# Attention and experts in one kernel: the order of the last tiles, single weight splits, halves at the end, later constants

## The chip, the cores and the metric

One core of one Trainium2 chip runs the kernel. The time is that of one execution in device microseconds. TensorE (PE) multiplies matrices, VectorE (DVE), ScalarE (ACT) and GpSimd (POOL) work on tiles, SyncE (SP) issues loads and stores. Names in brackets are those of the profile.

## The reference

Sliding window attention over 8 batches, 8 heads, 576 positions and head dimension 64, then a mixture of 8 experts over the 4608 tokens, one expert per token, and only for tokens whose skip score is positive:

```
scores = q @ k^T / 8            # where 0 <= i - j < 64, else -1e9
attn   = softmax(scores) @ v    # -> x, 4608 tokens x 512
keep   = x @ w_skip > 0
e      = argmax(x[keep] @ w_gate);  g = softmax(x[keep] @ w_gate)[e]
out    = x;  out[keep] += g * (relu(x[keep] @ w1[e]) @ w2[e])   # 512 -> 1024 -> 512
```

All inputs and outputs are float32.

## The kernel before, in words

The tokens are cut into 36 tiles of 128 (two blocks of 64 positions). A loop over the tiles is a software pipeline. For tile t+1 `score` writes the scores into `ps` (TensorE, line 259; for the first block of a sequence a band of large negative numbers goes ahead of them, line 245). VectorE masks them and takes the maximum (lines 276, 279), and ScalarE makes eight exponentials, one per head (`soften`, line 285); the second four of them are what `softened()` issues. For tile t TensorE transposes the exponentials (296), ScalarE and GpSimd make masked copies `ptm`, and for tile t-1 `tile_out` multiplies with the values (`av`, 444) and VectorE divides (455 to 458). The result x is stored and also transposed (`transpose_x`, 341, tile `px`), copied by ScalarE (346, `xt`) and multiplied with the router's weights (414); for the last tiles ScalarE copies these logits to `lg` (418). `route` then finds expert and gate on VectorE (gmx, gd, gfi, gfm, goh, gohb; 495 to 509), with one exponential on ScalarE (gex, 505), ranks the tokens with the constants `trib`, `cf`, `of` and `base`, and GpSimd scatters token numbers to `lists` in HBM (628).

The tokens of an expert form items, ten in all, of up to three tiles. An item runs in four steps over quarters of the hidden dimension. Per step, `up` makes the product `p` from x and the first weights (three matmuls per slice: high times high 860, low times high 861, high times low 862, here called by line only), ScalarE writes `hh` (917) and VectorE the rest `hl` (920). `down` multiplies with the second weights into `yv`, `yw` or `yu`. Every weight piece (128x1024) is loaded by SP as `raw` (790) and split in two: ScalarE casts the high half `whi` (809), VectorE subtracts to get the low half `wlo` (810). The splits run ahead of their use in a ring of ten; how far ahead, `expert_chunk` decides for each chunk of work with `weights_to(n)`, which issues splits until n pieces are split. At the end of an item `finish` multiplies by the gate and adds x (VectorE, 945), and GpSimd stores the rows indirectly (946). After the last item stands a loop over leftover slots (1395), which is skipped when there are none.

Each engine works through its instructions in the order in which the program wrote them. TensorE's instructions are fetched in blocks of 256, and `tick` counts them. Loads and stores of the attention stage are issued behind fixed instructions of TensorE, just behind the start of a block. The four constants of the router stand in `load_constants` (180 to 187) and are called once, in the loop at t = 1. The first q is loaded by SP behind the first k (1077), the band, the identity `identb` and others by ScalarE's queue (1079 to 1084). The first two items' chunks run in between the last attention tiles; the wait for `transpose_x` there is on the bank of the tile before, since `px` alternates between two banks of tag "t" and the logits of line 414 stand in the same bank as `px`.

Of the kernel before, what the change touches and what calls it, by code (L numbers as in the profile page):

```python
# [10 lines left out]
F32 = mybir.dt.float32  # L11
# [38 lines left out]
AHEAD = 5  # L50
FLYING = 6
# [101 lines left out]
def window_attention_moe(ctx: ExitStack, tc, a, out):  # L153
# [58 lines left out]
    def load_q(n, s=0, e=4):  # L212
# [3 lines left out]
        return nc.sync.dma_start(qs[n][:, s:e], a["qT"][b, :, 4 * g + s : 4 * g + e])  # L216
# [20 lines left out]
    def score(t):  # L237
# [3 lines left out]
        for hf, (_, i) in enumerate(tiles[t]):  # L241
            if i == 0:
                for z in range(2):
                    h = slice(64 * z, 64 * z + 64)
                    tick(2, nc.tensor.matmul(
                        ps[64 * hf : 64 * hf + 64, z, :, 0:64],
                        identb[h, h],
                        band[h].unsqueeze(1).to_broadcast([64, 4, 64]),
                        start=True,
                        stop=True,  # L250
                        skip_group_check=True,
                    ))
        for p in range(4):
            for hf, (_, i) in enumerate(tiles[t]):
                for z in range(2):
# [10 lines left out]
                    ))  # L266
        ss[t] = ps
# [301 lines left out]
    def tick(n, ins):  # L569
        pe[0] += n  # L570
        if pe[0] >= pe[1]:
# [3 lines left out]
            transfers(ins)  # L575
        return ins
# [282 lines left out]
    def mm3(o, lh, ll, rh, rl, first, last):  # L859
        nc.tensor.matmul(o, lh, rh, start=first, stop=False)  # L860
        nc.tensor.matmul(o, lh, rl, start=False, stop=False)  # L861
        nc.tensor.matmul(o, ll, rh, start=False, stop=last)  # L862
# [79 lines left out]
    def finish(y, xg, idx, gate, n=1):  # L942
        m, w = y.shape
        yo = hpool["y"].tile([P, w], F32, name=f"yo{n}", bufs=3 if n == 1 else 1)[:m]
        nc.vector.scalar_tensor_tensor(yo, y, gate, xg[:m], op0=ALU.mult, op1=ALU.add)  # L945
# [12 lines left out]
    def down(it, qi, wh, wl, tags="u", ends=None):  # L958
# [8 lines left out]
        def add(j, f):  # L967
            r = slice(j * P, j * P + it.rows[j])
            w = slice(f * D, (f + 1) * D)
            mm3(it.ys[j], hh[:, f, r], hl[:, f, r], wh[:, w], wl[:, w],  # L970
# [497 lines left out]
```

## Time and profile before

| | us |
|---|---|
| three runs | 416.78, 414.01, 413.55 (median 414.01) |
| profiled execution | 408.61 |
| its span | 407.0 |
| TensorE busy in it | 376.0 |
| VectorE, ScalarE, GpSimd busy | 270.8, 224.4, 178.2 |
| mean granted clock of TensorE | 0.997 |

The profiled execution is one run of its own: 1.61 us lie around its span, and it is 5.4 us shorter than the median of the three runs. TensorE's busy time does not tell how full it is inside a busy stretch, since matmuls overlap; the idle time ahead of an instruction, in brackets behind it, is what can be read. "issue" there means that the profile shows nothing that the engine waited for.

### The profile page before, as it was taken

Reading aid. Unit: us, or ns where it says so; the run is one execution under the profiler, and the core shown is the slowest. Engines: PE = TensorE matmul, PEld = TensorE weight load, DVE = VectorE, ACT = ScalarE, POOL = GpSimd, SP = SyncE. Lnnn points to the kernel's source line nnn. Section 1 sums busy time; section 2 is a strip of 40 time slices with the busy share of each in tenths; the row PEclk is TensorE's granted clock in tenths of the full one; section 3 lists DMA queues with packets and bytes.
Section 4 is the critical chain, followed back from the end, with each engine's and each line's share of the span. In section 5 each row is a group of like instructions: output and inputs, shape, how many; then the busy total and the mean of one; then the engine's idle time right before and its main releaser. Section 6 shows DMA issues by size and latency. Waiting matters only on the chain. (4 is left out here: it accounts for less than half of the span.)

```text
span 407.0 us, 13642 instructions
## 1 busy us (share of the span) xinstructions
PE 376.0 (92%) x5425; PEld 318.1 (78%) x5425; DVE 270.8 (67%) x552; ACT 224.4 (55%) x643; POOL 178.2 (44%) x222
## 2 busy tenths in 40 slices
PE   4879898989889997999999999999999999999993
PEld 3667787767676866898788898888889889888872
DVE  2667778868688856797616789764555566764591
ACT  3767787767667865564315646334425344452670
POOL 5545445467767583475262718116106423010121
PEclk9999999999999999999999999999999999999998
DMA  8988889869877798668738866657657776685460
GB/s 271 321 278 272 284 266 316 299 216 289 279 241 215 220 340 294 200 202 297 275 115 276 263 194 204 209 174 235 217 161 249 262 238 188 207 250 174 156 230 28
DMA packets 40677, 95.68 MB, mean 235 GB/s; under 512 B 7216, under 2 KB 9021, under 8 KB 40604
## 3 DMA queue, kind: packets, MB, share of 16 engines
q1 hardware_dynamic: 33124, 78.21, 59.3%
q0 software_dynamic: 4896, 10.02, 7.5%
q10 hardware_dynamic: 2592, 6.57, 4.8%
q8 instruction: 43, 0.70, 0.7%
q14 instruction: 22, 0.18, 0.1%
HBM read 80.57 MB, written 14.91 MB: 235 GB/s over the span
## 5 line engine op out<-in xcount | busy, mean ns | idle before, releaser
L810 DVE TENSOR_TENSOR wlo<-raw,whi 128x1024 fp32r<-128x1024 f32 x72 | 86.5, 1222 | 24.2 <-ACT whi L809 22.2
L917 ACT ACTIVATE hh<-p 128x256 fp32r<-128x256 f32 (+4 forms) x56 | 22.5, 403 | 94.4 <-PE p L862 91.8
L809 ACT CAST whi<-raw 128x1024 fp32r<-128x1024 f32 x72 | 73.7, 1049 | 0.0
L303 POOL TENSOR_TENSOR ptm<-pm,mask 128x512 f32<-128x512 f32 x36 | 45.9, 1275 | 53.8 <-ACT pm L302 53.6
L860 PE MATMUL p<-x,whi 128*128 128x288 f32 (+5 forms) x224 | 67.4, 301 | 1.8 <-DVE hl L920 1.3
L862 PE MATMUL p<-x,wlo 128*128 128x288 f32 (+5 forms) x224 | 66.0, 295 | 0.6 <-DVE wlo L810 0.6
L861 PE MATMUL p<-x,whi 128*128 128x288 f32 (+5 forms) x224 | 65.8, 294 | 0.0
L285 ACT ACTIVATE s<-ps,nmx 128x64 f32<-128x64 f32 x288 | 62.8, 329 | 1.2
L946 POOL DMA_INDIRECT out<-yo,les x15 | 15.4, 1029 | 95.3 <-DVE yo L945 88.0
L444 PE MATMUL av<-vm,ptm 64*64 64x65 f32 x2048 | 47.4, 223 | 9.2 <-issue 9.1
L920 DVE SCALAR_TENSOR_TENSOR hl<-p,hh 128x256 fp32r<-128x256 f32 (+4 forms) x56 | 24.8, 444 | 46.3 <-ACT hh L917 26.8
L444 PEld LDWEIGHTS av<-vm,ptm 64*64 64x64 f32 x2048 | 39.6, 134 | 16.3 <-issue 14.9
L628 POOL DMA_INDIRECT lists<-ent,gdi x36 | 38.3, 1063 | 19.9 <-issue 12.6
L860 PEld LDWEIGHTS p<-x,whi 128*128 128x128 f32 x224 | 42.2, 188 | 4.7 <-DVE hl L920 1.9
L861 PEld LDWEIGHTS p<-x,whi 128*128 128x128 f32 x224 | 42.2, 188 | 0.9
L862 PEld LDWEIGHTS p<-x,wlo 128*128 128x128 f32 x224 | 42.2, 188 | 0.8 <-DVE wlo L810 0.8
L259 PE MATMUL ps<-k,q 64*64 64x128 f32 (+1 forms) x1024 | 38.5, 274 | 0.9 <-DMA q<-qT 0.4
L276 DVE COPY_PREDICATED ps<-sel,ps 128x512 f32<-128x512 int32 x36 | 24.9, 690 | 18.2 <-PE ps L259 14.0
L346 ACT COPY xt<-px 128x512 f32<-128x512 f32 x36 | 21.2, 589 | 23.8 <-PE px L341 17.6
L259 PEld LDWEIGHTS ps<-k,q 64*64 64x64 f32 x1024 | 31.0, 138 | 4.3 <-issue 2.2
L860 PE MATMUL yv<-whi,hh 128*128 128x512 f32 (+1 forms) x72 | 28.8, 400 | 0.0
L862 PE MATMUL yv<-whi,hl 128*128 128x512 f32 (+1 forms) x72 | 28.2, 392 | 0.0
(188 smaller groups left out, 741.7 us busy)
## 6 DMA issues: line engine op xcount, KB each, us to landing
raw<-wq SPq DMA_DIRECT2D x72, 512.0 KB
vm<-vp SPq DMA_DIRECT2D x32, 260.0 KB
q<-qT SPq DMA_DIRECT2D x32, 256.0 KB
out<-x SPq DMA_DIRECT2D x32, 256.0 KB
k<-kT SPq DMA_DIRECT2D x24, 256.0 KB
w<-wq ACTq DMA_DIRECT2D x12, 512.0 KB
k<-kT SPq DMA_DIRECT2D x8, 384.0 KB
kt<-kT SPq DMA_DIRECT2D x8, 256.0 KB
```

The costliest lines, as they stand in the source:

```text
L259: tick(4, nc.tensor.matmul(ps[64 * hf : 64 * hf + 64, z, p, 64 * w.start :], q[h, p], k[h, w, p], start=True, stop=True, skip_group_check= ...
L276: nc.vector.copy_predicated(cur, sel.unsqueeze(1).unsqueeze(1).to_broadcast([P, 2, 4, 64]), ps[..., :64])
L285: nc.scalar.activation(s[:, q, z], cur[:, z, q], AF.Exp, bias=nmx[:, z, q : q + 1], scale=0.125)
L303: nc.gpsimd.tensor_tensor(part(0, 2), split(pm[:, 0:2], 2), kept(2), op=ALU.mult)
L444: ins = tick(4, nc.tensor.matmul(av[64 * hf : 64 * hf + 64, z, q * VW : (q + 1) * VW], ptm[h, q, 2 * hf + 1 - w], win[hf][w][h, q], start= ...
L628: ins = nc.gpsimd.indirect_dma_start(out=lists, out_offset=bass.IndirectOffsetOnAxis(ap=di, axis=0), in_=ent.bitcast(I32), in_offset=None, ...
L809: nc.scalar.copy(hi, raw)
L810: nc.vector.tensor_tensor(lo, raw, hi.bitcast(F32), op=ALU.subtract)
L860: nc.tensor.matmul(o, lh, rh, start=first, stop=False)
L861: nc.tensor.matmul(o, lh, rl, start=False, stop=False)
L862: nc.tensor.matmul(o, ll, rh, start=False, stop=last)
L920: beat(nc.vector.scalar_tensor_tensor(hl[:, f, :m], p1[:, :m], 0.0, hh[:, f, :m].bitcast(F32), op0=ALU.max, op1=ALU.subtract))
```

## The change

Five things are altered.

1. The first q goes out on ScalarE's queue, first there, and the band on SP's; for tile 0 the band's matmuls stand behind the scores.
2. `load_constants` is a generator. From the fourth block on, `tick` takes one load of it at each block boundary: cf, the lists' zeros, of, trib. GpSimd's copy of `base` moves from t = 5 to t = 10.
3. At t = 34 the second four exponentials stand behind the cast of the first item's x and the copy of the logits. The first weight split of the stage stands ahead of the transpose of tile 33, and the last two transposes write to a bank of their own ("late", tag "u").
4. In `expert_chunk` the lead of the splits is bounded: a chunk splits what it needs now and otherwise one piece at most, and where the ring is short nothing but what it needs now.
5. The last step of the last item makes its output in two halves of 256 columns. Each half is multiplied by the gate as soon as it is there, and one store follows both.

```diff
     def load_constants():
-        nc.sync.dma_start(cf, a["c_f"])
-        nc.sync.dma_start(of, a["c_first"])
-        nc.sync.dma_start(trib, a["c_tri"])
-        nc.sync.dma_start(
+        yield nc.sync.dma_start(cf, a["c_f"])
+        yield nc.sync.dma_start(
             lists[:LPAD].rearrange(...), a["c_list"].rearrange(...),
         )
+        yield nc.sync.dma_start(of, a["c_first"])
+        yield nc.sync.dma_start(trib, a["c_tri"])
+
+    constant = load_constants()
...
+        if t:
+            banded()
         for p in range(4):
...
+        if not t:
+            banded()
...
-        px = psum.tile([P, NDC, P], F32, name="px", tag="t", bufs=2)
+        if t < NT - 2:
+            px = psum.tile([P, NDC, P], F32, name="px", tag="t", bufs=2)
+        else:
+            px = banks["late"].tile([P, NDC, P], F32, name="px", tag="u", bufs=1)
...
             transfers(ins)
+            if pe[1] > FETCH + QUIET * BLOCK:
+                load = next(constant, None)
+                if load is not None:
+                    behind(load, ins)
...
-        nc.vector.scalar_tensor_tensor(yo, y, gate, xg[:m], op0=ALU.mult, op1=ALU.add)
+        c = slice(0, w) if half is None else slice(half * w // 2, (half + 1) * w // 2)
+        nc.vector.scalar_tensor_tensor(yo[:, c], y[:, c], gate, xg[:m, c], op0=ALU.mult, op1=ALU.add)
+        if half == 0:
+            halved.append(yo)
+            return
...
-            for j in range(it.nt):
+            for half in range(2):
                 for f in range(2):
-                    add(j, f)
-                finish(it.ys[j], it.xg[j], it.idx[j], it.gate[j])
+                    add(0, f, half)
+                finish(it.ys[0], it.xg[0], it.idx[0], it.gate[0], half=half)
...
-        for f in (load_k, load_q):
-            after_load(f(0, 0, 2), 1)
-        nc.scalar.dma_start(band, a["c_band"])
+        after_load(load_k(0, 0, 2), 1)
+        after_load(load_q(0, 0, 2, nc.scalar), 1)
+        nc.sync.dma_start(band, a["c_band"])
...
-            if t == 1:
-                load_constants()
-            if t == 5:
+            if t == 10:
                 nc.gpsimd.tensor_copy(base, cf[:, off["base"]])
...
-                softened()
+                if t < NT - 2:
+                    softened()
                 if t >= FIRSTX:
                     its[0].split(xhl[0], t - FIRSTX, "t")()
                 if t - LAG[t] >= SINGLY:
                     logits(t - LAG[t])
+                if t == NT - 2:
+                    softened()
...
-                eager = 0 if short[0] or gathered[0] < 3 else min(ptr["split"] + RATE, ptr["free"] + min(RING, len(ring)) - 1)
-                weights_to(max(need, eager))
+                lead = ptr["free"] + min(RING, len(ring)) - 1 if gathered[0] >= 3 else need + 2
+                weights_to(now if short[0] else max(now, min(lead, ptr["split"] + RATE)))
...
-        transpose_x(NT - 3)
         weight_split(ptr["split"])
         ptr["split"] += 1
+        transpose_x(NT - 3)
```

On ScalarE, at t = 34, the eight exponentials `s` of the last tile stood ahead of the cast of x and the logits' copy `lg`; then came the copy `xt` of tile 33 and the first split of the stage. Before:

```order
L285 ACTIVATE s<-ps,nmx 128x64 x8
L850 CAST x_150<-px_3691 128x4x128
L418 COPY lg<-px 128x9
L346 COPY xt_3618<-px 128x4x128
L809 CAST whi_146<-raw_140 128x1024
L418 COPY lg<-px 128x9
```

Now:

```order
L294 ACTIVATE s<-ps,nmx 128x64 x4
L866 CAST x_150<-px_3687 128x4x128
L430 COPY lg<-px 128x9
L294 ACTIVATE s<-ps,nmx 128x64 x4
L825 CAST whi_146<-raw_140 128x1024
L358 COPY xt_3618<-px 128x4x128
L430 COPY lg<-px 128x9
```

Four exponentials, and the copy `xt`, have moved behind.

On VectorE, between the products' rests `hl` of the first item and its next x, the low halves of the third and fourth piece stood ahead of the router's work on the last group of tiles (`gmx` to `gohb`). Before:

```order
L920 SCALAR_TENSOR_TENSOR hl<-p_3921,hh 128x256
L810 TENSOR_TENSOR wlo_3719<-raw_142,whi_3718 128x1024
L810 TENSOR_TENSOR wlo_3721<-raw_143,whi_3720 128x1024
L920 SCALAR_TENSOR_TENSOR hl<-p_3948,hh 128x256
L495 TENSOR_REDUCE gmx<-lg 128x6
L497 TENSOR_TENSOR gd<-lg,gmx 128x48
L500 SCALAR_TENSOR_TENSOR gfi<-gd,cf 128x48
L502 TENSOR_REDUCE gfm<-gfi 128x6
L507 TENSOR_TENSOR goh<-gfi,gfm 128x48
L509 SCALAR_TENSOR_TENSOR gohb<-lg,goh 128x48
```

Now:

```order
L936 SCALAR_TENSOR_TENSOR hl<-p_3921,hh 128x256
L936 SCALAR_TENSOR_TENSOR hl<-p_3942,hh 128x256
L507 TENSOR_REDUCE gmx<-lg 128x6
L509 TENSOR_TENSOR gd<-lg,gmx 128x48
L512 SCALAR_TENSOR_TENSOR gfi<-gd,cf 128x48
L514 TENSOR_REDUCE gfm<-gfi 128x6
L519 TENSOR_TENSOR goh<-gfi,gfm 128x48
L521 SCALAR_TENSOR_TENSOR gohb<-lg,goh 128x48
L826 TENSOR_TENSOR wlo_3719<-raw_142,whi_3718 128x1024
L869 TENSOR_TENSOR x_3992<-px_4025,x_3992 128x4x128
L826 TENSOR_TENSOR wlo_3721<-raw_143,whi_3720 128x1024
```

The low half of the third piece has moved behind six of the router's operations, that of the fourth behind the rest of x. On ScalarE the two casts moved in the same way: behind `hh`, `lg` and `gex`. Further on, where four casts in a row stood between two pairs of `hh`, there are three, since three earlier ones have closed up.

At the very end, the loop over leftover slots (the rows with a jump, and the body ahead of them) stands between the last item's work and the program's end. GpSimd has the last item's store, from `yo_6648`, behind the loop both before and now:

```order
L1395 REGISTER_ALU
L1395 COMPARE_AND_BRANCH
L1395 UNCONDITIONAL_BRANCH
L946 DMA out<-yo_6648,les 4608x512
L1465 UNCONDITIONAL_BRANCH
```

VectorE, which before had the whole product ahead of the loop and nothing behind it, now has the second half's product there:

```order
L967 SCALAR_TENSOR_TENSOR yo_6850<-yu,lel,xg_115 128x512
L1422 REGISTER_ALU
L1422 COMPARE_AND_BRANCH
L1422 UNCONDITIONAL_BRANCH
L967 SCALAR_TENSOR_TENSOR yo_6648<-yv,les,xg_118 104x256
L1492 UNCONDITIONAL_BRANCH
```

The first half's product stays ahead of the loop. The four loads of constants stood in a row on SP's queue between loads of q and of vm; each now stands alone, the first of them thirteen rows of that queue further on, with four or five rows between two of them. TensorE's order is otherwise as it was, but for tile 0 and the twelve matmuls of half width.

## Rows read from the trace of the kernel before

**Rows 1.** The page's busy time: engine, us, share of the span, instructions.

```profile
PE 376.0 (92%) x5425; PEld 318.1 (78%) x5425; DVE 270.8 (67%) x552; ACT 224.4 (55%) x643; POOL 178.2 (44%) x222
```

**Rows 2.** Busy time by stage: window, busy us (instructions) by engine, clock, DMA share, GB/s.

```profile
20.00:30.00 10.00, 7.55 (x251) 6.36 (x251) 6.49 (x14) 6.90 (x28) 4.02 (x5) 1.00 0.80 266
...
150.00:160.00 10.00, 7.78 (x221) 6.53 (x213) 6.51 (x17) 6.15 (x20) 5.21 (x7) 1.00 0.95 348
...
160.00:170.00 10.00, 8.84 (x133) 7.90 (x134) 6.39 (x19) 4.71 (x10) 3.09 (x3) 1.00 0.77 249
...
200.00:300.00 100.00, 99.60 (x627) 87.22 (x627) 59.91 (x106) 41.95 (x74) 39.33 (x56) 1.00 0.65 210
```

**Rows 3.** TensorE's waits: what waited, for what; us in total, times, longest.

```profile
PE av L444 <- issue: 10.0, 19, 2.1
...
PE px L341 <- DVE hl L920: 0.5, 1, 0.5
...
PE p L860 <- issue: 0.5, 1, 0.5
```

**Rows 4.** The start, in order of time: start us, us, engine, line, operation, tiles, count [idle].

```profile
4.57 0.42 PE L245 MATMUL ps<-band,identb 64*64 64x256 bf16 x2 [4.57 <-DMA identb<-c_identb]
...
7.08 1.88 PE L259 MATMUL ps<-k,q 64*64 64x128 f32 x32 [0.43 <-DMA q<-qT]
```

**Rows 5.** In order of time, SP's queue and TensorE, 17 to 24 us.

```profile
17.14 0.83 SPq L184 DMA_DIRECT2D lists<-c_list  x1
...
23.24 0.40 PE L444 MATMUL av<-vm,ptm 64*64 64x65 f32 x13 [2.12 <-issue]
```

**Rows 6.** In order of time, ScalarE and TensorE at the transition, 154 to 161 us.

```profile
154.20 1.75 ACT L285 ACTIVATE s<-ps,nmx 128x64 f32<-128x64 f32 x8
...
154.90 0.64 PE L414 MATMUL px<-wg,xt 128*64 128x9 f32 x16
...
156.37 0.17 ACT L418 COPY lg<-px 128x9 f32<-128x9 f32 x1
...
156.59 0.66 PE L341 MATMUL px<-ident,x 128*128 128x128 f32 x4 [1.05 <-ACT lg L418]
...
160.12 0.39 PE L862 MATMUL p<-x,wlo 128*128 128x256 f32 x1 [0.57 <-DVE wlo L810]
```

**Rows 7.** In order of time, the third split and what reads it, 169 to 174 us.

```profile
169.16 2.00 ACT L809 CAST whi<-raw 128x1024 fp32r<-128x1024 f32 x2
...
171.57 0.17 ACT L418 COPY lg<-px 128x9 f32<-128x9 f32 x1
...
172.13 0.28 PE L862 MATMUL p<-x,wlo 128*128 128x256 f32 x1
...
172.86 0.19 DVE L495 TENSOR_REDUCE gmx<-lg 128x6 f32<-128x48 f32 x1
...
173.33 0.25 ACT L505 ACTIVATE gex<-gd 128x48 f32<-128x48 f32 x1 [1.59 <-DVE gd L497]
```

**Rows 8.** In order of time, four low halves in a row, 192 to 198 us.

```profile
192.86 4.63 DVE L810 TENSOR_TENSOR wlo<-raw,whi 128x1024 fp32r<-128x1024 f32 x4 [0.51 <-ACT whi L809]
...
197.88 0.40 PE L860 MATMUL p<-x,whi 128*128 128x288 f32 x1 [0.88 <-DVE hl L920]
```

**Rows 9.** The end; VectorE's drain behind the loop; an earlier product and its store.

```profile
399.13 0.39 PE L860 MATMUL yv<-whi,hh 128*104 128x512 f32 x1
...
400.71 0.75 DVE L945 SCALAR_TENSOR_TENSOR yo<-yv,les,xg 104x512 f32<-104x512 f32 x1 [2.02 <-PE yv L862]
...
402.73 1.02 POOL L946 DMA_INDIRECT out<-yo,les  x1 [5.82 <-issue]
...
L1465 DVEq DRAIN  x2: 10/14/17, 403.2 to 406.4; - x2
...
243.89 0.75 DVE L945 SCALAR_TENSOR_TENSOR yo<-yw,les,xg 128x512 f32<-128x512 f32 x1
...
244.94 1.15 POOL L946 DMA_INDIRECT out<-yo,les  x1 [4.68 <-DVE yo L945]
```

More of the change, by code (lines that the diff above doesn't have):

```diff
@@ L50 @@
 AHEAD = 5
+QUIET = 3
 FLYING = 6
@@ L210, in load_k, with load_q @@
         return nc.sync.dma_start(ks[n % NKB][:, s0 : e + 1], a["kT"][b, :, 4 * g + s0 - 1 : 4 * g + e])
-    def load_q(n, s=0, e=4):
+    def load_q(n, s=0, e=4, queue=nc.sync):
         b, g = divmod(n, 2)
@@ L240, in score, with banded @@
         win = windows(t)
[L241 to L252, printed above, removed]
+        def banded():
+            for hf, (_, i) in enumerate(tiles[t]):
+                if i == 0:
+                    for z in range(2):
+                        h = slice(64 * z, 64 * z + 64)
+                        tick(2, nc.tensor.matmul(
+                            ps[64 * hf : 64 * hf + 64, z, :, 0:64],
+                            identb[h, h],
+                            band[h].unsqueeze(1).to_broadcast([64, 4, 64]),
+                            start=True,
+                            stop=True,
+                            skip_group_check=True,
+                        ))
+        if t:
+            banded()
         for p in range(4):
@@ L857, in split_x, with mm3 @@
         return rest
[L859 to L862, printed above, removed]
+    def mm3(o, lh, ll, rh, rl, first, last, **kw):
+        nc.tensor.matmul(o, lh, rh, start=first, stop=False, **kw)
+        nc.tensor.matmul(o, lh, rl, start=False, stop=False, **kw)
+        nc.tensor.matmul(o, ll, rh, start=False, stop=last, **kw)
     class Item:
@@ L940, in up, with finish @@
             yield 1.3
-    def finish(y, xg, idx, gate, n=1):
+    halved = []
+    def finish(y, xg, idx, gate, n=1, half=None):
         m, w = y.shape
-        yo = hpool["y"].tile([P, w], F32, name=f"yo{n}", bufs=3 if n == 1 else 1)[:m]
-        nc.vector.scalar_tensor_tensor(yo, y, gate, xg[:m], op0=ALU.mult, op1=ALU.add)
+        if half:
+            yo = halved.pop()
+        else:
+            yo = hpool["y"].tile([P, w], F32, name=f"yo{n}", bufs=3 if n == 1 else 1)[:m]
+        c = slice(0, w) if half is None else slice(half * w // 2, (half + 1) * w // 2)
[3 more added lines that the diff above has]
+            return
         ins = nc.gpsimd.indirect_dma_start(
@@ L965, in down, with add @@
                 it.ys.append(y[: it.rows[j]] if j < it.full else y[:, 0:P])
-        def add(j, f):
+        def add(j, f, half=None):
             r = slice(j * P, j * P + it.rows[j])
-            w = slice(f * D, (f + 1) * D)
-            mm3(it.ys[j], hh[:, f, r], hl[:, f, r], wh[:, w], wl[:, w],
-                qi == 0 and f == 0, qi == NQ - 1 and f == 1)
+            c = slice(0, D) if half is None else slice(half * D // 2, (half + 1) * D // 2)
+            w = slice(f * D + c.start, f * D + c.stop)
+            mm3(it.ys[j][:, c], hh[:, f, r], hl[:, f, r], wh[:, w], wl[:, w],
+                qi == 0 and f == 0, f == 1 and qi == NQ - (2 if it is its[-1] and half is None else 1), **({} if half is None else {"skip_group_check": True}))
         if qi == NQ - 1 and it is its[-1]:
             tables["more"] = nc.values_load(tables["left"][0:1, 0:1], min_val=0, max_val=NSLOT)
-            for j in range(it.nt):
+            for half in range(2):
                 for f in range(2):
-                    add(j, f)
-                finish(it.ys[j], it.xg[j], it.idx[j], it.gate[j])
+                    add(0, f, half)
+                finish(it.ys[0], it.xg[0], it.idx[0], it.gate[0], half=half)
             return
```

2 lines of the change are left out of this document (1 added, 1 removed).

## The prediction

> **What bounds the kernel now.** The page's busy line comes first: TensorE works 376.0 us of the 407.0 us span [rows 1], so 31 us of idle TensorE are all that a reordering can win, and no instruction of weight is taken away here. The table by stage says where those 31 us lie [rows 2]. From 200 to 300 us TensorE is busy for 99.60 of 100 us, and the 100 us after it read the same, so the long expert stage has nothing to give. Idle time sits at the start, in the attention stage (7.55 of 10 us busy at 20 to 30), at the transition from attention to experts (7.78 and 8.84 of 10 us between 150 and 170), and behind the last matmul. The granted clock is 1.00 in every one of these windows, so no term below is a matter of the clock. The list of TensorE's waits [rows 3] then names the largest: "issue" ahead of the attention-times-values matmuls, 10.0 us in 19 pieces, the longest 2.1 us, which leaves a mean of (10.0 - 2.1) / 18 = 0.44 us for the others. These pieces come once per block of 256 of TensorE's instructions. Two waits of 0.5 us, for hl and before a product of the first expert item, lie in the transition.
>
> **The start.** TensorE first moves at 4.57 us, when the identity for the band arrives, and the scores follow [rows 4]. Now the scores stand first and q goes out on ScalarE's queue as its first load, instead of second on SP's. What the scores need, k and q, is 512 KB with the same bytes in flight, so they can begin about 0.2 us earlier at best. But the second tile's scores wait for their own q until 7.08 us [rows 4], and nothing puts that load ahead of where it was. I take -0.1 us, bounds -0.3 (band and identity wholly off the path) and +0.2 (q second to land because two queues share the engines).
>
> **The constants.** Four loads stand on SP's queue one behind the other, the last, the lists, issued at 17.14 for 0.83 us [rows 5]. From their shapes they are 256, 83, 32 and 32 KB. At the 266 GB/s of the window at 20 to 30 us [rows 2], 403 KB are 1.5 us of transfers. TensorE's longest pause, 2.12 us, ends at 23.24 [rows 5], and I read it as the fetch of instructions that stood behind them. If it falls to about 1.0, because q, k and v loads still queue there, 1.1 us go. Given back: the four loads now stand behind one fetch boundary each, cf, then the lists, the other two. The lists alone are 256 KB / 266 GB/s = 1.0 us of the queue, just before a later fetch; the small ones cost 0.1 to 0.3 us each. I take 0.6 us of new pauses, less than the 1.5 us of bytes because each comes alone: -1.1 + 0.6 = -0.5 us. Bounds: -1.7 (the pause falls to the mean 0.44 and nothing comes back) and +0.8 (nothing goes, the lists and the small ones lengthen later pauses by 0.8). GpSimd's copy of the base moves five tiles later with cf and still stands well ahead of the router that reads it: nothing.
>
> The row shows the longest pause right behind the loads, and shows no more than that. The Trainium skill, "DMA: Bandwidth & Descriptors", section "Queues, rings and completion order", says that each DMA engine takes turns between the queue rows it has work for, a packet from each; "Runtime: NRT & Kernel Launch", section "Instruction fetch mechanics", calls the crossing of a block "mostly hidden". By these an instruction fetch on its own queue would not stand behind SP's loads, this term would be 0 and the sum -0.5.
>
> **The transition, tile 34.** Before, all eight exponentials run on ScalarE from 154.20 for 1.75 us; then the cast of x and the copy of the logits (156.37), and only behind that copy could TensorE transpose the next x, at 156.59 after 1.05 us idle [rows 6]. Now the second four exponentials (0.87 us) stand behind cast and copy, and the transpose has a bank of its own. Cast and copy move up by 0.87 us, but the logits' matmuls end at 154.90 + 0.64 = 155.54 [rows 6], so I move the transpose to 155.83: -0.76. The weight split now stands ahead of the transpose's copy, so the wait for the low half at 160.12 (0.57) falls to about 0.3: TensorE is 1.02 ahead. The two waits of 0.5 us [rows 3] stood for hl, made late by the same work, and go too: 2.0 us ahead. Followed through by hand in the new order, with the transposes out of the way of the tile before, it is 2.36 us just before 169.1.
>
> **One split per chunk.** The four splits that stood in pairs come one at a time. The third split's cast ran at 169.16 as one of two (2.00 us for both, so 1.00 each), and TensorE read its low half at 172.13 [rows 7]. Now it stands on ScalarE behind hh, the logits' copy and the router's exponential, and on VectorE behind six router operations. The logits' copy of the last tile, at 171.57 [rows 7] before, comes at 169.2 by the gain above. From there 0.17 for the copy, then two small VectorE operations and ScalarE's exponential, 0.72 us from 172.86 to 173.58 as they followed each other before [rows 7], then 1.00 for the cast and 1.16 for the low half (4.63 / 4 [rows 8]), with a tenth between them: 172.35. TensorE, 2.36 us ahead, is stopped, and goes on 0.2 us later than before. So the whole gain of the paragraph above is lost again here: +0.2 net. VectorE's next work, hl of that step, is not late by it, since it stands ahead of the split.
>
> Further on the four casts in one block, with the low halves from 192.86 to 197.49 [rows 8], become three. hl waits behind them, and TensorE 0.88 us for hl at 197.88 [rows 8]. One low half less is 1.16 us, more than the wait: -0.88. The transition gives +0.2 - 0.9 = -0.7. Bounds: -3.3, if the split is not late, and +0.6, if the transpose did not hang on the copy and only a third of the 0.88 goes. From 200 us on each step has work for a split in its shadow, and the order there is unchanged: 0.
>
> **The end.** The last six matmuls start at 399.13 and VectorE's product waits for them until 400.71, 1.58 us; it takes 0.75 [rows 9]. In halves the first six take half the columns: 0.85, so the first product starts at 399.98 and takes 0.45 (between 0.38, half of 0.75, and 0.75). But the second half shares the bank and waits for it, and VectorE's second product stands behind the branch that skips the loop. Before, VectorE's product ended at 401.46 and its next instruction behind the loop came at 403.2 [rows 9]: 1.74 us. So the second product starts at 400.43 + 1.74 = 402.17 and ends 402.6. GpSimd's store follows its product by 0.30 us where it waits for one (243.89 + 0.75 to 244.94) [rows 9]: 402.9, against 402.73. +0.2 us; bounds 0 and +0.6 (first product 0.75).
>
> **Sum.** -0.1 - 0.5 - 0.7 + 0.2 = -1.1 us against the profiled execution's own 408.61 us (its span 407.0), so 407.5. The median of the three runs, 414.01, stands 1.3% above that execution; I carry the same amount over: 413.0 (rounded up from 412.9).
>
> **Rivals.**
> *Late split with no lead.* If the transpose waited at 156.59 for the logits' matmuls and not for ScalarE, TensorE has no 2.36 us to lose. The chain from the copy at 171.57 then lands at 171.57 + 0.17 + 0.72 + 2.16 + 0.1 = 174.72 instead of 172.13: +2.6; with the burst's -0.9 and the end's +0.2 that is +1.9, or 415.9, and 416.7 if the constants cost their worst. For it speaks that the copy at 156.37 stood behind two things, matmuls and cast; against it, that those matmuls had ended 0.8 us before [rows 6]. It decides if TensorE's transpose of tile 33 stays within 0.2 us of its old distance to the exponentials. Chance 0.2, and 0.05 of it beyond +1%, by pauses that pile up.
> *Waits gone for good.* The split finds room and the 2.36 us stay: -3.3, with constants -1.7, start -0.3 and end +0.2: -5.1, or 408.9. The windows at 150 to 170 us hold 3.4 us of idle time in all [rows 2], so nothing larger is to be had. Against it: the order of both engines puts the split last. Chance 0.15.
> *Fetches do not hang on the loads.* A pause ends with the arrival of instructions, and the loads beside it are coincidence: constants 0, the rest as summed, -0.6, or 413.4. Chance 0.2: the long pause stands once, just there, which speaks against it; the two sections above speak for it.
> The forecast has 0.45.
>
> **Range and chances.** One per cent is 4.1 us, about what a measurement of this kernel can tell from no change. The forecast's own bounds with the spread of the three runs (413.55 to 416.78) give 411 to 415; to the rivals on both sides it reaches 409.5 to 416.3. Only the second rival, with its terms near their ends, lies below 409.9: faster 0.15. Beyond 418.1 lies the late split with everything else at its worst: slower 0.05. The rest, 0.80, is within one per cent.
>
> **What would show it.** Right: the pause near 23 us falls to about 1 us while one near 43 grows; the transpose follows the logits' matmuls at once; TensorE stands idle some 2.5 us before the first product with the third split's low half; the wait at 197.88 is gone; VectorE's second product starts about 1.74 us behind the end of its first. Wrong: TensorE between 160 and 180 us as full as at 200, a longest pause that stays at 2 us, or a second product within 0.5 us of the last matmul's data.

## The result, and the profile after

The change is slower. In the runs taken against the kernel before its ratio is 1.0137, 95% interval 1.0099 to 1.0176; the median of its six runs is 416.88 us (416.27 to 419.65), against 413.73 us (411.46 to 416.78) for six of the kernel before. A ratio leaves out the runs that lie more than 1.5% above the fastest of their kernel, a median counts them all. The plain ratio of these medians is 1.0076 and that of the means 1.0092, so the 1.0137 is rather high. Taken again in two later studies, it gave 1.0074 (1.0042 to 1.0105) and 1.0097 (1.0062 to 1.0131). The forecast was 413.0 us with a range to 416.3; the time lies just above that range.

The profiled execution took 416.83 us, its span 415.2. That is 8.2 us over the 407.0 of the kernel before, more than the runs' ratio gives: that kernel alone has medians of 407.2 us in some studies below and 413.3 in others, so only distances inside one trace are compared. The page's busy line hardly moves, 379.6 us for TensorE instead of 376.0:

```profile
PE 379.6 (91%) x5431; PEld 325.1 (78%) x5431; DVE 271.5 (65%) x553; ACT 225.1 (54%) x643; POOL 181.9 (44%) x222
```

The table by stage, with the columns of [rows 2] (the clock stands third from the end):

```profile
20.00:30.00 10.00, 9.25 (x295) 8.11 (x292) 8.17 (x19) 7.70 (x31) 4.73 (x5) 1.00 0.87 282
150.00:160.00 10.00, 7.77 (x209) 6.63 (x203) 6.69 (x18) 6.34 (x21) 5.42 (x7) 0.90 0.91 313
160.00:170.00 10.00, 10.00 (x139) 9.75 (x137) 5.89 (x16) 3.30 (x9) 2.04 (x2) 0.76 0.61 206
170.00:180.00 10.00, 7.04 (x52) 6.36 (x51) 5.48 (x12) 4.84 (x10) 7.53 (x8) 0.75 0.37 108
180.00:190.00 10.00, 10.00 (x66) 9.10 (x66) 8.06 (x25) 5.04 (x10) 5.73 (x6) 0.91 0.62 200
190.00:200.00 10.00, 10.00 (x64) 9.25 (x64) 9.51 (x18) 7.45 (x11) 5.62 (x4) 1.00 0.90 305
200.00:300.00 100.00, 98.61 (x621) 86.70 (x620) 60.59 (x109) 41.16 (x73) 40.30 (x57) 1.00 0.65 214
```

Two things are new. The clock, 1.00 in every window of [rows 2], is 0.75 to 0.91 in four windows between 150 and 190 us: a window that reads "10.00 busy" at 0.76 is not a full window. And 170 to 180 us holds 3 us of idle time. TensorE's list of waits names it:

```profile
PE av L456 <- issue: 10.8, 17, 1.7
...
PE p L876 <- ACT whi L825: 2.5, 1, 2.5
...
PE px L865 <- DMA xg<-out,les: 1.1, 1, 1.1
...
PE px L353 <- ACT lg L430: 0.9, 1, 0.9
...
PE p L878 <- DVE wlo L826: 0.5, 1, 0.5
```

The wait for whi, the cast of a split, is in no list of TensorE's waits of the kernel before. In order of time, ScalarE, VectorE and TensorE around it (compare [rows 7]):

```profile
171.54 0.64 PE L426 MATMUL px<-wg,xt 128*64 128x9 f32 x16
172.11 0.66 PE L865 MATMUL px<-ident,xg 128*128 128x128 f32 x4
173.35 0.17 ACT L430 COPY lg<-px 128x9 f32<-128x9 f32 x1 [1.32 <-PE px L865]
174.03 0.24 ACT L517 ACTIVATE gex<-gd 128x48 f32<-128x48 f32 x1 [0.51 <-DVE gd L509]
174.18 1.03 ACT L825 CAST whi<-raw 128x1024 fp32r<-128x1024 f32 x1
175.24 1.23 DVE L826 TENSOR_TENSOR wlo<-raw,whi 128x1024 fp32r<-128x1024 f32 x1 [0.27 <-ACT whi L825]
175.26 0.58 PE L876 MATMUL p<-x,whi 128*128 128x256 f32 x1 [2.49 <-ACT whi L825]
176.52 0.58 PE L878 MATMUL p<-x,wlo 128*128 128x256 f32 x1 [0.46 <-DVE wlo L826]
```

The split's cast starts at 174.18, behind the logits' copy and the router's exponential, and TensorE stands still for 2.49 us, makes two products with the high half, and stands still for 0.46 more, for the low half. Single microseconds tell what comes behind that stop:

```profile
174.00:175.00 1.00, 0.00 (x0) 0.00 (x0) 0.84 (x4) 0.97 (x2) 0.99 (x1) 0.99 0.00 0
175.00:176.00 1.00, 0.74 (x2) 0.50 (x2) 0.76 (x1) 1.00 (x3) 0.69 (x2) 0.50 0.03 1
...
180.00:181.00 1.00, 1.00 (x7) 1.00 (x7) 0.59 (x1) 0.86 (x2) 0.70 (x2) 0.50 0.77 226
181.00:182.00 1.00, 1.00 (x7) 1.00 (x6) 1.00 (x2) 0.00 (x0) 1.00 (x1) 0.59 0.60 231
```

For the 6 us behind the stop TensorE runs at the lower level, 1.2 GHz (0.50), with seven matmuls in a full microsecond. The same fall stands from 158 to 164 us, behind the wait at tile 33. There, in order of time (compare [rows 6]):

```profile
154.60 0.93 ACT L294 ACTIVATE s<-ps,nmx 128x64 f32<-128x64 f32 x4
155.30 0.64 PE L426 MATMUL px<-wg,xt 128*64 128x9 f32 x16
156.66 0.17 ACT L430 COPY lg<-px 128x9 f32<-128x9 f32 x1 [0.65 <-PE px L426]
156.72 0.94 ACT L294 ACTIVATE s<-ps,nmx 128x64 f32<-128x64 f32 x4
156.88 0.66 PE L353 MATMUL px<-ident,x 128*128 128x128 f32 x4 [0.94 <-ACT lg L430]
```

Four exponentials are indeed gone from in front of the copy, yet ScalarE now stands 0.65 us idle for the matmuls, and the transpose comes 1.58 us behind the logits' start instead of 1.69 [rows 6].

The start (compare [rows 4, 5]) and the end (compare [rows 9]), in order of time:

```profile
4.72 1.34 PE L266 MATMUL ps<-k,q 64*64 64x64 f32 x26 [4.72 <-DMA q<-qT]
...
9.13 1.47 PE L305 MATMUL pt<-ident,s 128*128 128x128 f32 x4 [0.96 <-DMA ident<-c_ident]
...
18.79 0.74 PE L456 MATMUL av<-vm,ptm 64*64 64x65 f32 x35 [1.52 <-issue]
...
23.09 0.40 PE L456 MATMUL av<-vm,ptm 64*64 64x65 f32 x13 [0.75 <-issue]
...
406.11 0.28 PE L876 MATMUL yv<-whi,hh 128*104 128x256 f32 x1
...
407.01 0.48 DVE L967 SCALAR_TENSOR_TENSOR yo<-yv,les,xg 104x256 f32<-104x256 f32 x1 [1.34 <-PE yv L878]
...
409.20 0.48 DVE L967 SCALAR_TENSOR_TENSOR yo<-yv,les,xg 104x256 f32<-104x256 f32 x1 [1.71 <-PEq L1422]
409.99 1.03 POOL L971 DMA_INDIRECT out<-yo,les  x1 [6.11 <-DVE yo L967]
```

### The profile page after: what moved, and what is told of

Its sections match the earlier page's. It is cut to its first block, busy times and chain, and to the rows that moved or that the text cites. A ratio compares the mean times of both kernels' runs of the same rounds, so it can differ in the third digit from the quotient of the medians.

```text
span 415.2 us, 13659 instructions
## 1 busy us (share of the span) xinstructions
PE 379.6 (91%) x5431; PEld 325.1 (78%) x5431; DVE 271.5 (65%) x553; ACT 225.1 (54%) x643; POOL 181.9 (44%) x222
## 5 line engine op out<-in xcount | busy, mean ns | idle before, releaser
L876 PE MATMUL p<-x,whi 128*128 128x288 f32 (+5 forms) x224 | 69.0, 308 | 2.5 <-ACT whi L825 2.5
L878 PE MATMUL p<-x,wlo 128*128 128x288 f32 (+5 forms) x224 | 67.6, 302 | 0.5 <-DVE wlo L826 0.5
L877 PE MATMUL p<-x,whi 128*128 128x288 f32 (+5 forms) x224 | 67.4, 301 | 0.0
L644 POOL DMA_INDIRECT lists<-ent,gdi x36 | 40.5, 1125 | 21.2 <-issue 14.4
L876 PEld LDWEIGHTS p<-x,whi 128*128 128x128 f32 x224 | 43.9, 196 | 4.5 <-ACT whi L825 2.7
L877 PEld LDWEIGHTS p<-x,whi 128*128 128x128 f32 x224 | 43.9, 196 | 0.9
L878 PEld LDWEIGHTS p<-x,wlo 128*128 128x128 f32 x224 | 43.7, 195 | 0.8 <-DVE wlo L826 0.8
L876 PE MATMUL yv<-whi,hh 128*128 128x512 f32 (+2 forms) x74 | 29.3, 395 | 0.6 <-DVEq L1422 0.6
L878 PE MATMUL yv<-whi,hl 128*128 128x512 f32 (+2 forms) x74 | 28.6, 386 | 0.0
```

What stands on the lines that cost most here:

```text
L644: ins = nc.gpsimd.indirect_dma_start(out=lists, out_offset=bass.IndirectOffsetOnAxis(ap=di, axis=0), in_=ent.bitcast(I32), in_offset=None, ...
L876: nc.tensor.matmul(o, lh, rh, start=first, stop=False, **kw)
L877: nc.tensor.matmul(o, lh, rl, start=False, stop=False, **kw)
L878: nc.tensor.matmul(o, ll, rh, start=False, stop=last, **kw)
```

## The experiments

**Theory.** The third split, placed behind the router (the "late split"; "early" is its old place), stops TensorE, and the lower clock behind the stop makes it dearer. **Rivals:** the constants' loads or the start; the end in halves ("whole" is the old form); the tile-34 order itself.

The runs form five studies; each ratio is to the kernel before in the same study. That kernel took 407.2 us in the first two studies and 413.3, 413.2 and 412.3 in the others (medians).

**First study: one part undone or alone.** `e1` is the change with the split back ahead of the router:

```diff
-                weights_to(now if short[0] else max(now, min(lead, ptr["split"] + RATE)))
+                weights_to(need if short[0] else max(now, min(lead, ptr["split"] + RATE)))
```

> The changed kernel, with the third and fourth split back ahead of the router's work on the last tiles (where the ring is short a chunk splits what the next one needs, as before the change); all else as changed. Late-split theory: the 2.49 us wait for the third split's high half and the 0.46 us for its low half go, TensorE has no pause long enough for the clock to fall at 175 us, and the kernel is 4 to 6 us faster than the change, 411 to 413 us beside a before of 413.7. Rival, the clock falls at the transition whatever the split does (it also fell at 158 us, ahead of the split): the wait goes, the time falls by 1 to 2 us only, 415 to 416. Rival, the loss comes from start, constants or end: no more than 1 us.

`e2` is the kernel before with the late split alone:

```diff
-                weights_to(max(need, eager))
+                weights_to(now if short[0] else max(need, eager))
```

> The kernel before with the late split alone: where the ring is short a chunk splits only what it needs now. Late-split theory: slower than before by 2.5 us of waiting and up to 3.5 us for the clock behind it, 416 to 420 us, with a pause of 2 to 5 us ahead of the third split's first product. Rivals (clock falls anyway, or other parts): within 1.5 us of before.

`e3` is the kernel before with the constants taken one per block, `e4` the change with its last output in one piece:

```diff
-            if t == 1:
-                load_constants()
-            if t == 5:
+            if t == 10:
...
+            if pe[1] > FETCH + QUIET * BLOCK:
+                load = next(constant, None)
```

> The kernel before with the four constants' loads alone moved, one per block, and the base's copy at tile 10. The forecast's term: 0.5 us faster, the pause near 23 us at about 1 us. If fetches do not hang on loads: within 0.2 us of before, the long pause still there or elsewhere. If it is a part of the loss: 1 us or more slower. From the delays read in the two traces (the attention stage 0.7 to 1.4 us ahead from tile 7 to tile 32): 0.7 to 1.4 us faster.

```diff
-            for half in range(2):
-                for f in range(2):
-                    add(0, f, half)
-                finish(it.ys[0], it.xg[0], it.idx[0], it.gate[0], half=half)
+            for f in range(2):
+                add(0, f)
+            finish(it.ys[0], it.xg[0], it.idx[0], it.gate[0])
```

> The changed kernel with the last output in one piece as before. From the trace of the change, whose second product started at 409.20, 1.71 us behind the end of the first: 0.5 to 1.5 us faster than the change, 415.5 to 416.5 us. If the halves gained: slower than the change.

Measured: `e1` 1.0032 (0.9982 to 1.0082), `e2` 1.0050 (1.0007 to 1.0094), `e3` 0.9957 (0.9894 to 1.0020), `e4` 1.0023 (0.9977 to 1.0069). The late split alone makes the kernel before slower; the constants don't. Undoing the split took the wait for whi away, but `e1` did not become faster than before. Its list of TensorE's waits shows another one further on:

```profile
PE px L865 <- DMA xg<-out,les: 2.3, 1, 2.3
```

By single microseconds, with the clock third from the end:

```profile
205.00:206.00 1.00, 0.21 (x1) 0.22 (x2) 0.00 (x0) 0.00 (x0) 0.00 (x0) 0.93 0.25 81
206.00:207.00 1.00, 1.00 (x6) 1.00 (x6) 0.00 (x0) 0.09 (x1) 0.42 (x3) 0.50 0.00 0
207.00:208.00 1.00, 1.00 (x6) 1.00 (x6) 0.47 (x1) 0.50 (x1) 0.36 (x3) 0.50 0.05 16
```

There too the clock falls behind the stop. TensorE waits for the gather of the third item's rows, which GpSimd issues behind the load of its list; that list comes from the scatters behind the router.

**Second study.** `e5` is the change once more, without an edit. `e6` has the edits of `e1` and `e4` together. `e7` fills the stop: the transposes ahead of it are made six times over, with the same output. The condition also held at two later items, where they are plain extra work. `e8` is the kernel before with the halves alone.

> The change itself, unaltered, beside the others of this call on one chip. If the loss on the first chip (ratio 1.0137) is the kernel's: 1.008 to 1.018. From the two single parts measured so far (late split alone 1.005, the change with a whole end 1.0023): 1.005 to 1.008.

> The change with both undone: third and fourth split early again and the last output in one piece; what stays is the first q, the constants, tile 34 and one split per chunk. If late split and halves are the loss: no slower than before, ratio 0.994 to 1.001, about 4 us faster than the change. If start or tile 34 lose as well: over 1.002.

```diff
-        for c in range(NDC):
+        for c in (i % NDC for i in range(NDC * (6 if xg is its[1].xg[0] else 1))):
```

> The change with the wait for the third split filled: the four transposes of the second item's first tile are made six times over into the same place, 20 matmuls of some 0.12 us in the 2.5 us in which TensorE had nothing. If the half clock behind the wait costs time: TensorE stays at 1.00 between 174 and 182 us, what was 6.4 us at half clock runs in 3.2, and the kernel is 2 to 3 us faster than the change although it does more. If only the wait costs: the same as the change within 0.5 us.

```diff
...
-            for j in range(it.nt):
+            for half in range(2):
                 for f in range(2):
-                    add(j, f)
-                finish(it.ys[j], it.xg[j], it.idx[j], it.gate[j])
+                    add(0, f, half)
+                finish(it.ys[0], it.xg[0], it.idx[0], it.gate[0], half=half)
```

> The kernel before with the last output in halves alone. From the two traces: from VectorE's last hl to the end of the span the change took 1.2 us more, so 1.0 to 1.3 us slower than before, 1.0025 to 1.003. The forecast's term: 0.2 us slower, 1.0005. If overlapping the halves gains: faster.

Measured: `e5` 1.0074 (1.0042 to 1.0105), `e6` 1.0035 (0.9999 to 1.0071), `e7` 1.0080 (1.0042 to 1.0118), `e8` 1.0041 (1.0008 to 1.0075). The halves alone cost time, though the interval comes close to 1. `e7` decides nothing, since it carries the later extra work. `e6` waits 2.5 us for the same gather.

**Third study.** `e9` fills the stop once only. `e10` is the kernel before with the new start, `e11` with the tile-34 order, `e12` with one split per chunk but the third one early.

```diff
+    filled = []
...
-        for c in range(NDC):
+        more = 1 if xg is not its[1].xg[0] or filled else 6
+        filled.extend([0] * (more - 1))
+        for c in (i % NDC for i in range(NDC * more)):
```

> The change with the filling of the wait for the third split at that one place only (the kernel before this repeated it at two later items, where 40 matmuls cost 2 to 5 us of a full TensorE). If the half clock behind the wait costs time: 1.5 to 3 us faster than the change, ratio to before 1.000 to 1.004, unless TensorE then waits longer for the third item's gather near 205 us, which would leave 1.003 to 1.006. If the half clock costs nothing: 1.0074 as the change.

```diff
-        for f in (load_k, load_q):
-            after_load(f(0, 0, 2), 1)
-        nc.scalar.dma_start(band, a["c_band"])
+        after_load(load_k(0, 0, 2), 1)
+        after_load(load_q(0, 0, 2, nc.scalar), 1)
+        nc.sync.dma_start(band, a["c_band"])
```

> The kernel before with the start alone: first q by ScalarE's queue, band by SP's, tile 0's band behind its scores. The forecast's term: 0.1 us faster, lost in the noise (0.998 to 1.002). From the traces of the change, where the first transposes waited 0.96 us for the identity and the clock fell right behind: 0.5 to 1.5 us late at tile 3, made up by tile 10 since loads set the pace there, so also 0.998 to 1.002. If it persists: 1.003.

```diff
+            px = banks["late"].tile([P, NDC, P], F32, name="px", tag="u", bufs=1)
...
-                softened()
+                if t < NT - 2:
+                    softened()
...
+                if t == NT - 2:
+                    softened()
...
-        transpose_x(NT - 3)
         weight_split(ptr["split"])
         ptr["split"] += 1
+        transpose_x(NT - 3)
```

> The kernel before with the last tiles' order alone: second four exponentials of the last tile behind cast and logits' copy, split ahead of the transpose, own bank for the last two transposes. The forecast's terms: up to 2.4 us ahead when the third split is read, and that stands early here, so 1.5 to 2.4 us faster, 0.994 to 0.997. If TensorE then waits for the third item's gather, which GpSimd's scatters set: 0.998 to 1.002, with a wait of 2 us or more ahead of that item's transposes.

```diff
-                weights_to(max(need, eager))
+                weights_to(need if short[0] else max(now, min(lead, ptr["split"] + RATE)))
```

> The kernel before with one split per chunk alone, but with what the next chunk needs where the ring is short, so that the third split stays early. The forecast's term: the wait of 0.88 us for hl near 198 us goes, 0.9 us faster, 0.998. If the gather near 205 us sets the pace: the same as before, 0.998 to 1.002, the wait moved there.

Measured: `e9` 1.0090 (1.0045 to 1.0135), `e10` 0.9989 (0.9949 to 1.0028), `e11` 0.9939 (0.9895 to 0.9982), `e12` 1.0009 (0.9965 to 1.0054). In this study the tile-34 order is the one part with a gain that can be told from nothing. In `e9` the clock holds through the place where it fell. In order of time, TensorE there:

```profile
175.83 2.84 PE L869 MATMUL px<-ident,xg 128*128 128x128 f32 x24
179.00 0.39 PE L880 MATMUL p<-x,whi 128*128 128x256 f32 x1 [0.33 <-issue]
180.26 0.39 PE L882 MATMUL p<-x,wlo 128*128 128x256 f32 x1 [0.76 <-DVE wlo L826]
```

And by single microseconds:

```profile
175.00:176.00 1.00, 1.00 (x21) 0.84 (x20) 0.21 (x1) 0.38 (x1) 0.69 (x2) 1.00 0.46 146
...
181.00:182.00 1.00, 1.00 (x11) 1.00 (x11) 0.94 (x1) 0.25 (x1) 0.69 (x2) 1.00 0.78 131
```

The fall follows this stop: behind it the clock is at 0.50 in the traces of all seven kernels with the late split and no filling, and at 1.00 at that place in `e7`, `e9` and all eleven with the split early. The runs of `e9` do not show the gain, however. Its ratio, 1.0090, is not below the 1.0074 that its expectation gave for a clock that costs nothing; but the interval, 0.45% to either side or 1.9 us, is too wide to tell that from the 1.5 us which the traces give. What the clock alone costs rests on traces and stays open in the runs.

**Fourth study.** `e13` is the kernel before with constants and tile-34 order (the edits of `e3` and `e11`), `e14` is `e6` again, `e15` the kernel before with tile-34 order and late split (`e11` and `e2`), `e16` the change a third time.

> The kernel before with the two parts that gained alone, the constants one per block (0.9957) and the last tiles' order (0.9939); splits, start and end as before. If the gains add: 0.988 to 0.993. If both only bring TensorE earlier to the third item's gather: 0.994 to 0.997, as the better one. If they were chance: 0.998 to 1.002.

> The change with the third and fourth split early and the last output in one piece, a second time, on the chip of the others of this call. If 1.0035 was right: 1.001 to 1.006, and one split per chunk takes back what the last tiles' order gives. If the parts add (start 0.9989, constants 0.9957, tile 34 0.9939, one split 1.0009): 0.988 to 0.994.

> The kernel before with the last tiles' order and the late split, nothing else. If the late split, bound to the router's chain, takes whatever lead TensorE has and adds its wait: 1.003 to 1.008, 0.9 to 1.4 per cent above the last tiles' order alone. If the two are independent: 0.9939 x 1.005 = 0.999.

> The change itself once more, beside these: 1.007 to 1.014, as on the first two chips. If late split and halves are its loss, it stands 0.6 to 1.2 per cent above the kernel with both undone.

Measured: `e13` 0.9976 (0.9942 to 1.0010), `e14` 1.0003 (0.9974 to 1.0033), `e15` 1.0063 (1.0024 to 1.0102), `e16` 1.0097 (1.0062 to 1.0131). The tile-34 order with the late split is slower than the kernel before, where two independent parts would have given 0.999; in the same study `e13`, with the split early, is not. By their single ratios the start, the constants, the tile-34 order and single splits (third one early) would give 0.989 together. `e6` and `e14`, which have these four, are at 1.0035 and 1.0003: most of what the parts seem to gain is not there in their sum, and no run shows why. The change loses 0.94% against `e14`, which differs from it by the split and the halves alone. In `e15`, where the clock was whole until the stop, the list of TensorE's instructions has the pattern of the change:

```profile
170.07 0.64 PE L417 MATMUL px<-wg,xt 128*64 128x9 f32 x16
...
173.82 0.58 PE L863 MATMUL p<-x,whi 128*128 128x256 f32 x1 [2.52 <-ACT whi L812]
...
175.08 0.58 PE L865 MATMUL p<-x,wlo 128*128 128x256 f32 x1 [0.46 <-DVE wlo L813]
```

**Fifth study.** `e17` is `e11` again, `e18` is `e4` again.

> The last tiles' order alone on the kernel before, a second time, as the version that would beat both kernels. If 0.9939 was right: 0.990 to 0.997. If it was chance, as the 0.9976 with the constants suggests: 0.997 to 1.001.

> The change with the last output in one piece but the third split late, a second time. If the late split on top of the last tiles' order costs 0.6 to 1.2 per cent and the halves the rest of the change's loss: 1.004 to 1.007, between the change (1.0097) and the change with both undone (1.0003). If the halves are all of it: 0.999 to 1.002.

Measured: `e17` 0.9953 (0.9909 to 0.9996), `e18` 1.0076 (1.0034 to 1.0118). The gain of the tile-34 order is not safe. `e11` has it in ratio and medians (411.27 against 413.25), but the medians of `e17` and of the kernel before beside it, 412.29 and 412.28, are the same, and the interval of `e13` reaches 1.0010. With the whole output and the late split the kernel is slower here; as `e4` the same program had 1.0023 (0.9977 to 1.0069), which left that open.

**The transition in distances.** Each is the difference of two start times in one trace, in us: from the logits' matmuls of tile 33 to those of the last tile (A), from these to the logits' copy (B), from that copy to the first product with a low half behind the stop (C), from there to the sixth hl of the expert stage (D), from the third hl to the sixth (E), from the sixth to the twentieth (F).

| | A | B | C | D | E | F |
|---|---|---|---|---|---|---|
| before | 15.87 | 0.80 | 0.56 | 4.92 | 8.39 | 54.33 |
| the change | 16.24 | 1.81 | 3.17 | 6.14 | 12.46 | 54.81 |
| `e16`, the change | 14.02 | 1.81 | 3.17 | 6.09 | 12.42 | 54.92 |
| `e5`, the change | 16.67 | 0.69 | 3.16 | 6.37 | 11.57 | 54.84 |
| `e15`, tile 34 and late | 13.34 | 1.84 | 3.17 | 5.88 | 12.23 | 54.71 |
| `e9`, stop filled | 13.90 | 1.83 | 3.17 | 4.60 | 10.94 | 54.33 |
| `e11`, tile 34 | 13.90 | 1.33 | | | 8.39 | 55.69 |
| `e6`, early, whole | 13.21 | 1.32 | | | 8.38 | 56.88 |
| `e12`, one split, early | 15.84 | 0.80 | | | 8.39 | 55.01 |

E is the clearest column. Its two ends before and in the change, VectorE in order of time:

```profile
168.66 0.42 DVE L920 SCALAR_TENSOR_TENSOR hl<-p,hh 128x256 fp32r<-128x256 f32 x1 [0.77 <-ACT hh L917]
...
177.05 0.41 DVE L920 SCALAR_TENSOR_TENSOR hl<-p,hh 128x256 fp32r<-128x256 f32 x1
```

```profile
170.20 0.42 DVE L936 SCALAR_TENSOR_TENSOR hl<-p,hh 128x256 fp32r<-128x256 f32 x1 [0.43 <-ACT hh L933]
...
182.66 0.42 DVE L936 SCALAR_TENSOR_TENSOR hl<-p,hh 128x256 fp32r<-128x256 f32 x1 [0.43 <-ACT hh L933]
```

In all eleven traces with the split early, the kernel before among them, it lies between 8.38 and 8.40; in the seven with the late split and no filling it lies between 11.52 and 12.61. That is 3.1 to 4.2 us more, and F gives nothing of it back in the rows above (in `e2` F is 53.41, beside 53.50 in `e3` of the same study).

## Why the prediction was wrong

**One split per chunk: the step that failed.** The forecast let the tile-34 order win 2.36 us and the late split lose it again, net +0.2. From the logits of tile 33 to the sixth hl it is +2.9 us in `e16`, which has a lead, and +5.2 in the change's own profile, which has none. The chain itself was right: it had 169.2 to 172.35, 3.15 us, for the way from the copy to the low half, and C is 3.17. The stop was foretold at "some 2.5 us" ahead of the low half; 2.49 stand ahead of the high half and 0.46 ahead of the low one. That the number agrees is in part luck: the same program as `e5` has 1.37 and 0.76. Three terms around it were missing or too small.

*The copy.* The forecast moved the copy with the logits, 0.80 behind them [rows 6, 7]. It comes 1.81 us behind them in the change, `e16` and `e15` (B), 0.68 to 0.69 in `e5`, `e4` and `e2`. From the logits to the low half the forecast's own numbers give 172.35 - (170.77 - 2.36) = 3.94 us, 170.77 being the logits' start before (171.57 less the 0.80); `e5` has 0.69 + 3.16 = 3.85, the change 1.81 + 3.17 = 4.98. Rows of `e5`, ScalarE and TensorE:

```profile
168.40 0.64 PE L426 MATMUL px<-wg,xt 128*64 128x9 f32 x16
169.09 0.17 ACT L430 COPY lg<-px 128x9 f32<-128x9 f32 x1 [0.20 <-PE px L426]
170.99 0.39 PE L876 MATMUL p<-x,whi 128*128 128x256 f32 x1 [1.37 <-ACT whi L825]
```

The same program, with the same work ahead, waits 1.37 us here and 2.49 there. The short form stood in both studies in which the kernel before took 407.2 us, the long one in the others; why is open. It is not the end of the transposes behind the logits: in `e9` there are six times as many, and the copy comes at the same 1.83.

*The clock.* "No term below is a matter of the clock" was read from windows of the kernel before, where the longest stop, 2.12 us [rows 5], lies in a window at 1.00. The stop of the new order did bring the clock down. From the low half to the sixth hl it now takes 5.88 to 6.37 us (D) instead of 4.92, that is +1.0 to +1.5, and 4.60 in `e9`, where the clock held. The granted clock of the runs agrees for the kernels of one study: a mean of 0.981 in `e15` and `e16`, 0.989 in the kernel before and in `e13`; 0.008 of 413 us is 3.3 us, as much as 6.6 us at half the clock would take away. In the first study it does not: `e2` and `e4` have 0.988 as a mean of their runs, so the fall of their profiles (0.977 and 0.972) is not in each run there, and the clock can't be the whole of the loss of `e2`. E of the change adds up: -0.77 (from the third hl to the logits, 1.34 instead of 2.11), + 3.62 (B and C together, 4.98 instead of 1.36), + 1.22 (D) = +4.07, and 12.46 - 8.39 = 4.07.

*The lead.* It exists where the clock holds: A is 1.85 to 2.66 us shorter in `e16`, `e11`, `e9`, `e15` and `e6`. Most of it is the waits that the forecast named: in `e16` the 0.57 for the low half [rows 6] and the two of 0.5 [rows 3] are gone, and one of 0.29 for xt is new (the second of the two was put down to issue, not to hl as the forecast has it). The 0.76 of the transpose came only in some traces. It stood 1.69 us behind the start of the logits before, and 1.56 to 1.72 in the change, `e9`, `e11`, `e13`, `e16` and `e17`, but 0.90 to 1.05 in `e1`, `e6`, `e7` and `e15`, where the copy came sooner. And in the profiled execution of the change the clock fell at 158 us and took the lead away: A is 16.24. That fall isn't the change's: A is 16.30 in `e17`, whose split is early, with 0.50 granted from 160 to 166 us, and `e2`, with tile 34 in the old order, has 0.50 from 151 to 160.

The three make up the error: from tile 33's logits to the sixth hl `e16` needs 25.09 us where the kernel before needed 22.15, +2.9 against +0.2, and of these 2.7 the copy is 1.0 (4.98 instead of 3.94), the clock 1.2 (D) and the shorter lead 0.5 (1.85 instead of 2.36).

**Rival 1** named this: a late split with no lead, 415.9 us, 416.7 at worst, chance 0.2. Its sign was met in the change (the transpose 2.28 us behind the exponentials' start, before 2.39, within 0.2), but with 2.42 it is met in `e16` too, where the lead is there: the sign does not tell the two cases apart. Its 415.9 lies 1.0 us under the median without a term for the clock, so that it comes so near is in part luck.

**The burst.** Right: the wait of 0.88 at 197.88 [rows 8] is gone, and 190 to 200 us is full. It is not kept: column F does not fall. TensorE now waits 1.1 us for the third item's gather. `e11` and `e6`, which reach that place sooner, wait 1.67 and 2.5 there, and their F is 1.4 and 2.6 us longer. That would return part of what the tile-34 order wins, but it is not shown: `e10`, whose way through the transition is the old one (A 15.80, E 8.40), waits as long, and its F is 55.92:

```profile
209.76 0.66 PE L855 MATMUL px<-ident,xg 128*128 128x128 f32 x4 [2.07 <-DMA xg<-out,les]
```

So the gather itself comes sooner or later from trace to trace, and why the parts don't add up stays open.

**The end.** The second product starts 1.71 us behind the end of the first (forecast 1.74). From the first of the last item's last matmuls to the store it is 3.88 us, before 3.60 [rows 9]: +0.28 (forecast +0.2). What the forecast left out comes after the store's start: 4.27 us to the end of the span before, 4.2 to 4.3 in all twelve traces of other kernels with a whole output, 4.82 to 5.21 in five of the seven with halves (the change 415.2 - 409.99 = 5.21). The other two, `e7` and `e9`, have halves and 4.29 and 4.28 (in `e9` the store starts at 412.52 and the span ends at 416.8). They differ from the change by extra transposes alone, so the halves by themselves do not make the late end. The term is +0.3 in these two and +0.8 to +1.2 in the five, instead of +0.2. `e8` has 1.0041, some 1.7 us, interval 0.3 to 3.1, which allows both. Why the end comes later in some is open.

**The constants.** The -0.5 is not to be seen. The pauses move: 1.52 at 18.79 and 0.75 at 23.09, where 2.12 stood at 23.24 [rows 5]. In the first study `e2` has the constants unmoved and pauses of 1.71, 1.32 and 1.35, so they wander without the move. The last scores start at 144.46 us in `e2` and, with the constants moved, at 144.69, 145.67 and 148.06 in `e3`, `e4` and `e1`. The rival that put this at 0 was nearer (without the term the forecast's sum is -0.6, as that rival has it; the -0.5 in its paragraph on queues and fetches is a slip); the runs of `e3` allow -1.1% to +0.2%, so a small gain stays open.

**The start.** TensorE's first work moved from 4.57 to 4.72, not ahead by 0.1; the scores, which stood behind the band at 4.68, by 0.04. That is inside the bounds. A new wait of 0.96 us for the transposes' identity came behind it, which no step had; the `e10` ratio of 0.9989 shows no cost.

**What is shown and what is argued.** Shown by runs: the late split costs 0.5 to 0.9% (`e2` alone; `e15` against `e13` in one study; the change against `e14`, with the halves), and the halves cost a little (`e8`, once). Seen once and not again in the medians: a gain of the tile-34 order (`e11`, `e17`). Shown by traces only: how the loss divides between stop, copy and clock. Open: why the four other parts together gain nothing. Each interval is 0.3 to 0.6% wide to either side. If one part is kept, it is the tile-34 order alone, which no run shows to be slower.

## What to carry to other kernels

A chain that starts at an engine's own work moves with that engine: here the split hangs on the logits that TensorE itself makes, so a lead of TensorE does not hide the wait (E is 12.42 with the lead and 12.46 without it). When an engine's stop is priced, price the work behind it too, at the lower clock, even if the trace before shows none. And gains that were measured one by one need not add up, so run the sum as well.

## What the runs showed of the hardware

- Behind a stop of TensorE of 2.5 us the granted clock was 0.50 for some 6 us of work, then 1.00; in `e5` the same fall came behind stops of 1.37 and 0.76. Behind the 2.12 us at 23.24 in the kernel before it stayed at 1.00. Behind a wait of about 1 us at tile 33 it fell in some executions (the change, `e13`, `e17`) and not in others (`e11`, `e16`), with waits of 0.92 to 1.08 us in all of them.
- ScalarE's copy of a TensorE result started 0.69 us behind the start of its matmuls in one study (`e5`) and 1.81 in others (the change, `e16`), in the same program.
- From the start of the last indirect store to the end of the span it was 4.2 to 4.3 us in fifteen traces, two of them (`e7`, `e9`) with its data made in two products, and 4.8 to 5.2 in the five others with two products.
